# Routing of a mixture of experts planned in two parts, behind an attention kernel

## The chip, the cores and the metric

The kernel runs on one core of a Trainium2 chip. The metric is the device time of one execution in microseconds (us). A core has five engines with an in-order queue each: TensorE (PE, matmuls; PEld is its weight load), VectorE (DVE), ScalarE (ACT), GpSimd (POOL) and SyncE (SP, which here only issues transfers). POOL issues transfers too, with the v loads, the expert weights, and the indirect gathers and scatters.

## The reference

Attention with rotary embedding on 8 batches x 8 heads x 576 tokens x 64, then a dense feed-forward plus, for each of the 4608 tokens, one of 8 experts, chosen by the largest logit and weighted by its probability:

```
q_rot, k_rot = (rotate(q), rotate(k))
scores = scale * np.matmul(q_rot, k_rot.transpose(0, 1, 3, 2))
...
x = np.ascontiguousarray(attn_out.transpose(0, 2, 1, 3)).reshape(B * S, H * D)
y_dense = np.maximum(x @ w1_dense, 0.0) @ w2_dense
expert_idx = np.argmax(x @ w_gate, axis=1)
...
    y_moe[mask] = gate_w[mask, None] * (np.maximum(x[mask] @ w1[e], 0.0) @ w2[e])
return (y_dense + y_moe).astype(np.float32)
```

## The kernel before

**Attention** works on 32 head pairs (NP), four to a batch (HP). In attention() (L466) the loop over pairs i has nine steps t. At step t PE computes the scores of pair i+2 (s1_block, L279) of which DVE takes row maxima (L293, negm), and the shifted scores of pair i (s2_strip, L319) of which ACT takes exponentials (L325). At t = 1, 4 and 6 PE multiplies the exponentials of pair i-1 with ones and with v (av_sums, av_tails, av_main), and DVE scales the result into xf (L365, L373). At t = 2 PE transposes the maxima of pair i+1 (L299, once for each pair), ACT and DVE make two rows mT of them, and SP writes these into the transposed q (L304); the next pair's shifted scores (L314) wait for that. At t = 2 also, rope runs for pair i+4 (stage_rope, L254): on DVE for the first four pairs, then on POOL in four operations (L263 to L266); SP transposes its result (L275). At t = 5 come the loads of q and k (SP), of v (POOL, two heads of each parity at a time), of the feed-forward's weights (POOL, L211): the dense ones at i = 8, one expert's first matrix at every odd i from 11, the second matrices w2e at i = 30 and 31, where the early pool has been given back. At i = 4 route_constants() (L174) builds constants on POOL, three DVE operations read the last of them (L195).

**Routing.** When a batch's four pairs are done, POOL casts xf to xb (L377, L379), PE makes the batch's logits (L389, L398), and gate() (L406) finds the chosen expert as a one-hot table hs and the weight gw on DVE and ACT, for the 5 strips of 128 tokens that a batch has (NS = 40 strips in all). rank() (L425) counts on DVE, with a matmul at its middle (L437, which waits for DVE's cnt, L435), the place of each token among those of its expert, and makes two tables lo for the plan. SP turns xb into rows (x_turn, L456) and writes rows and gw to the DRAM tile xd (x_store, L460); a row has 257 words.

**Plan and feed-forward.** After attention, routing() (L559) places the tokens of each expert in tiles of 128 rows, NT = 43 tiles in all: 80 small matmuls (L592) give for each tile the tokens to take (take_i) and to put (put_i), and woff the expert of each tile. ffn() (L678) runs over groups of 1, 2 and then 4 tiles. fetch() gathers each tile's rows from xd (POOL, L625) and SP transposes them (L628), two groups ahead; dense_in() (L631) computes the dense hidden layer of a group; expert_in, expert_turn and out_tile follow for each tile, the last two one and two tiles later. out_tile() sums the dense part in one PSUM tile and the expert part in another; ACT copies the first (L668), DVE adds the second times gw (L669), POOL scatters the rows to the output (L671).

**Order.** In attention the queues of PE, SP and POOL follow the order as written; those of DVE and ACT are ordered by a planner (L539). Plan: ordered by the planner. In the feed-forward all are as written (L708).

## Time and profile before

| | |
|---|---|
| median of 3 runs | 683.71 us (683.06 to 684.70) |
| the profiled execution | 688.99 us, span 687.3 us, mean granted PE clock 0.897 |
| PE busy | 489.6 us (71%) |
| DVE busy | 429.5 us (62%) |
| ACT busy | 319.0 us (46%) |
| POOL busy | 383.4 us (56%) |
| transfers | 83.50 MB, mean 121 GB/s |
| first L299 / last L299 (PE) | 39.1 us / 463.6 us |
| first dense matmul of the feed-forward (L636) | 514.8 us |

Busy times are sums over the instructions of an engine; the share is of the span. In the slices of the page each digit is the busy share of one fortieth of the span (17.2 us) in tenths, and PEclk is the clock that PE was granted, in tenths of full speed. In a list of waits a line has the waiting instruction, the one waited for, and the total time, the number and the longest of the waits. In a timeline a line has start, duration, engine, line, operation, tiles and shapes, and in brackets the idle time of the engine just before and what ended it. A window gives busy times, the clock, the share of the 16 transfer engines (it can be above 1, as packets overlap) and GB/s.

### The profile page before, as it was taken

To read this page: it belongs to the slowest core of one execution; us is meant where nothing else is said; L and a number is where in the kernel's file an instruction comes from. 1 tells how busy PE (TensorE), PEld (TensorE's weight loads), DVE (VectorE), ACT (ScalarE), POOL (GpSimd) and SP (SyncE) were. 2 spreads that over 40 slices of the span, in tenths; PEclk is the share of its full clock that TensorE was granted. 3 is DMA by queue.
4 is the path that set the end of the run, shared out by engine and by line. 5 is a ranking of instruction groups with operands and counts; after the bars stand their busy time and mean duration, and the time that the engine had idled before them with its cause. 6 is when DMAs were issued, how large, how long until landed. Compare 5 with 4: busy or idle time off the path is not lost. (4 is left out here: it accounts for less than half of the span.)

```text
span 687.3 us, 10849 instructions
## 1 busy us (share of the span) xinstructions
PE 489.6 (71%) x3777; PEld 246.1 (36%) x3777; DVE 429.5 (62%) x737; ACT 319.0 (46%) x644; POOL 383.4 (56%) x340
## 2 busy tenths in 40 slices
PE   0449867387488468738818955884628999999996
PEld 0114434143244234414404432441324444444442
DVE  8767747885987887788797789772341223323233
ACT  2007745265266337526715742763404445444542
POOL 6048959667936936966693595040134545555423
PEclk9999989699889869959977986997758999999999
DMA  8548754379777867577476865279237555546610
GB/s 198 96 91 153 134 108 94 63 164 153 117 146 146 148 127 133 113 122 169 90 149 135 156 115 94 37 122 196 40 81 146 131 139 150 149 125 131 138 62 1
DMA packets 185284, 83.50 MB, mean 121 GB/s; under 512 B 143152, under 2 KB 181552, under 8 KB 185232
## 3 DMA queue, kind: packets, MB, share of 16 engines
q1 hardware_dynamic: 156912, 53.55, 37.5%
q0 software_dynamic: 28320, 29.27, 23.4%
q8 instruction: 31, 0.51, 0.3%
q14 instruction: 21, 0.17, 0.1%
HBM read 52.86 MB, written 16.01 MB: 100 GB/s over the span
## 5 line engine op out<-in xcount | busy, mean ns | idle before, releaser
L293 DVE TENSOR_REDUCE negm<-s 128x1 f32<-128x576 f32 x288 | 210.6, 753 | 79.5 <-PE s L291 62.7
L325 ACT ACTIVATE pm<-s 128x512 f16<-128x512 f32 x288 | 163.3, 594 | 164.4 <-PE s L314 143.7
L291 PE MATMUL s<-qkT 128*128 128x288 bf16 x512 | 116.5, 313 | 34.1 <-DMA qkT<-nat 24.1
L314 PE MATMUL s<-qkT 128*128 128x64 bf16 (+1 forms) x512 | 114.1, 300 | 32.5 <-DMA qkT<-mT 19.3
L263 POOL TENSOR_TENSOR ra<-qk,cosx 128x1152 bf16<-128x1152 f32 x28 | 73.6, 2630 | 89.6 <-DMA qk<-in_k_dram 60.1
L671 POOL DMA_INDIRECT out_dram<-y,put_i x43 | 42.9, 997 | 77.6 <-DVE y L669 77.0
L291 PEld LDWEIGHTS <-qkT 128*128 128x128 bf16 x512 | 42.2, 102 | 89.6 <-issue 46.5
L377 POOL CAST xb<-xf 128x2048 bf16<-128x2048 f32 x8 | 15.1, 1892 | 98.3 <-DVE xf L373 98.3
L669 DVE SCALAR_TENSOR_TENSOR y<-ye,xg,y 128x512 f32<-128x512 f32 x43 | 32.3, 751 | 58.9 <-PE ye L666 33.9
L266 POOL TENSOR_TENSOR nat<-ra,rb 128x1152 bf16<-128x1152 bf16 x28 | 66.3, 2368 | 2.2
L656 DVE COPY he<-tr 128x512 bf16<-128x512 bf16 x43 | 18.2, 423 | 65.7 <-PE tr L654 59.1
L437 PE MATMUL pc<-cnt,tri 128*128 128x8 bf16 x8 | 1.5, 185 | 80.4 <-DVE cnt L435 80.4
L625 POOL DMA_INDIRECT xg<-xd,take_i x43 | 41.4, 963 | 28.1 <-issue 28.1
L314 PEld LDWEIGHTS <-qkT 128*128 128x128 bf16 x512 | 37.5, 100 | 42.8 <-DMA qkT<-mT 17.7
L648 ACT ACTIVATE hn<-pe 128x512 bf16<-128x512 f32 x43 | 25.7, 599 | 49.5 <-PE pe L646 21.2
L636 PE MATMUL pd<-xs,w1d 128*128 128x512 bf16 (+2 forms) x192 | 41.2, 370 | 8.5 <-DMA xs<-xg 7.8
L638 ACT ACTIVATE hd<-pd 128x512 bf16<-128x512 f32 (+2 forms) x48 | 26.4, 553 | 43.2 <-PE pd L636 42.8
L646 PE MATMUL pe<-w1e,xs 128*128 x172 | 45.0, 385 | 1.3 <-issue 1.3
L663 PE MATMUL yd<-w2d,hd 128*128 128x512 bf16 x172 | 44.1, 379 | 0.2
L666 PE MATMUL ye<-w2e,he 128*128 x172 | 44.1, 379 | 0.0
L344 PE MATMUL pz<-pm,ones 128*64 128x512 f16 x320 | 43.7, 406 | 0.0
L344 PE MATMUL px<-pm,v 128*64 128x512 f16 x320 | 41.8, 392 | 0.4 <-ACT lz L351 0.4
(159 smaller groups left out, 771.3 us busy)
## 6 DMA issues: line engine op xcount, KB each, us to landing
qk<-in_q_dram SPq DMA_DIRECT2D x32, 256.0 KB
qk<-in_k_dram SPq DMA_DIRECT2D x32, 256.0 KB
v<-in_v_dram POOLq DMA_DIRECT2D x32, 128.0 KB, 3.6
xd<-natx SPq DMA_DIRECT2D x8, 512.0 KB
w1e<-in_moe_w_dram POOLq DMA_DIRECT2D x8, 512.0 KB, 5.7
w2e<-in_moe_w_dram POOLq DMA_DIRECT2D x8, 512.0 KB, 11.1
qk<-in_q_dram SPq DMA_DIRECT2D x32, 32.0 KB
qk<-in_k_dram SPq DMA_DIRECT2D x32, 32.0 KB
```

The source lines that it names most:

```text
L263: eng.tensor_tensor(a, x, cx, AL.mult)
L266: eng.tensor_tensor(nat[:, :, :, 0:D], a, s, AL.add)
L291: nc.tensor.matmul(ps[:, c, 0:CH], lhsT=qT[:, t * P:(t + 1) * P], rhs=kT[:, k0 + c * CH:k0 + (c + 1) * CH], start=True, stop=True)
L293: nc.vector.tensor_reduce(state["negm", i][:, t:t + 1], ps[:, :, 0:CH], axis=AX.XY, op=AL.max, negate=True)
L314: nc.tensor.matmul(out_ap, lhsT=kT[:, s * P:(s + 1) * P], rhs=qT[:, qa if s < 4 else qb], start=True, stop=True)
L325: nc.scalar.activation(state["pm", i][:, s], ps, AF.Exp, scale=float(scale))
L344: nc.tensor.matmul(out_ap[64 * h:64 * h + 64], lhsT=lhsT, rhs=rhs, start=(n == 0), stop=(n == 4))
L625: nc.gpsimd.indirect_dma_start(out=xg[:, u, :], out_offset=None, in_=xd[:, :], in_offset=bass.IndirectOffsetOnAxis(ap=take_i[:, t:t + 1].b ...
L646: nc.tensor.matmul(ps, lhsT=xs[:, u, dt, :], rhs=w[:, 0, dt, :], start=(dt == 0), stop=(dt == DT - 1))
L663: nc.tensor.matmul(pd, lhsT=hd[:, ft, u], rhs=w2d[:, ft, :], start=(ft == 0), stop=(ft == FT - 1))
L666: nc.tensor.matmul(pe, lhsT=he[:, ft], rhs=w[:, 0, ft, :], start=(ft == 0), stop=(ft == FT - 1))
L671: put = nc.gpsimd.indirect_dma_start(out=out[:, :], out_offset=bass.IndirectOffsetOnAxis(ap=put_i[:, t:t + 1].bitcast(mybir.dt.uint32), ax ...
```

## The change

- logits_sum() only copies a batch's logits into a table lgs. gate() and rank() are replaced by gate_steps() and rank_steps(), each run twice: for the 30 strips of the first six batches, and for the 10 strips of the last two. The gate weight is split in three bf16 parts, which go through the plan's matmuls with the two parts of the token number (NPT = 5) and come out as gp for each tile row; xd loses its column of weights, and x_store two of its four transfers.
- plan_steps() plans T1 = 20 tiles, all full, from the first six batches, and then the remaining 23 from all that is left. The first gate, rank and plan are put into steps of pairs 29 to 32, with the gathers of the first four tiles at (32, 5); the second runs in the feed-forward, two steps to a tile. The matmuls with the tables number 30 and 40 in place of 80.
- Queues: in attention the order of DVE and ACT is now as written too. v is loaded a batch at a time (four transfers at i = 1, 5, ...), an expert's first matrix at every even i from 10, w2e at i = 29 to 31, x_turn of batch b at t = 8 of i = 4b + 6 and x_store at t = 8 of i = 4b + 7 (before: t = 3 of 4b + 5 and t = 7 of 4b + 6); those of the last batch stand behind the loop. The wa pool takes memory from the early pool.
- Feed-forward: groups of 1, 3, 4, 4, 4, 4 and then 4, 4, 4, 4, 4, 3 tiles; dense_in() of the next group is spread over the tiles of this one. The expert's hidden layer is scaled by gp at the ReLU on ACT, both products go into one PSUM tile, and DVE copies it.

```diff
--- before
+++ after
-    VB = 4
+    VB = 2
     v16s = []
     for i in range(VB):
-        t = const_p.tile([P, 2, 10, D], fp16, name=f"v16_{i}")
+        t = const_p.tile([P, HP, 10, D], fp16, name=f"v16_{i}")
...
+    SA = 5 * (B - 2)
+    NA = (B - 2) * S
-    XR = DG // 2 + 1
+    XR = DG // 2
     NT = N // P + E - 1
+    T1 = (NA - E * (P - 1) + P - 1) // P
+    T2 = NT - T1
...
+    lgs = route_p.tile([P, NS, E], f32)
+    groups = ((0, SA), (SA, NS))
...
+    NPT = 5
+    parts = route_p.tile([P, NS, NPT, 1], bf16)
...
-    def stage_v(g):
+    def stage_v(b):
...
+            heads = v[b, a::2]
...
     def logits_sum(b):
...
-        lg = ap.tile([P, 5, E], f32, tag="lg", bufs=1, name="lg")
-        nc.vector.memset(lg[TAIL:P, 4, :], 0.0)
-        nc.vector.tensor_copy(lg[:, 0:4, :], ps[:, 0:4, :])
-        nc.vector.tensor_copy(lg[0:TAIL, 4, :], ps[0:TAIL, 4, :])
-        gate(b, lg)
+        nc.vector.tensor_copy(lgs[:, 5 * b:5 * b + 4, :], ps[:, 0:4, :])
+        nc.vector.tensor_copy(lgs[0:TAIL, 5 * b + 4, :], ps[0:TAIL, 4, :])
...
+    def gate_steps(k, wp):
...
+        def a():
+            nc.vector.tensor_reduce(mx[:, :, 0], lg, axis=AX.X, op=AL.max)
+            nc.vector.tensor_tensor(ex, lg, mx.broadcast_to(sh), AL.subtract)
+        def b():
+            fb = first.rearrange("p j e -> p (j e)")[:, None, :].broadcast_to([P, n // 5, 5 * E])
+            nc.vector.scalar_tensor_tensor(hit.rearrange("p (b j) e -> p b (j e)", j=5),
+                                           in0=ex.rearrange("p (b j) e -> p b (j e)", j=5), scalar=0.0,
+                                           in1=fb, op0=AL.is_equal, op1=AL.mult)
+            nc.scalar.activation(ex, ex, AF.Exp)
+            nc.vector.tensor_reduce(top[:, :, 0], hit, axis=AX.X, op=AL.max)
+            nc.vector.tensor_scalar(top, top, scalar1=0.5, scalar2=None, op0=AL.max)
+        def c():
+            nc.vector.tensor_tensor(hs.rearrange("p e s -> p s e"), hit, top.broadcast_to(sh), AL.is_equal)
+            nc.vector.tensor_reduce(gw, ex, axis=AX.X, op=AL.add)
+            nc.vector.reciprocal(gw, gw)
+        def d():
+            nc.vector.tensor_copy(pt[0], gw)
+            nc.vector.tensor_tensor(gw, gw, pt[0], AL.subtract)
+            nc.vector.tensor_copy(pt[1], gw)
+            nc.vector.tensor_tensor(gw, gw, pt[1], AL.subtract)
+            nc.vector.tensor_copy(pt[2], gw)
+        return [a, b, c, d]
...
+    def rank_steps(k, wp, psum):
...
+        def a():
+            nc.vector.tensor_tensor_scan(run.rearrange("p e s -> p (e s)"),
+                                         keeps[k].rearrange("p e s -> p (e s)"),
+                                         hs.rearrange("p e s -> p (e s)"), 0.0, AL.mult, AL.add)
+            nc.vector.tensor_copy(cnt, run[:, :, n - 1])
+        def b():
+            pc = psum([P, 2, E, 1])
+            nc.tensor.matmul(pc[:, 0, :, 0], lhsT=tri, rhs=cnt, start=True, stop=(k == 0))
+            for x in range(k):
+                nc.tensor.matmul(pc[:, 0, :, 0], lhsT=ones_b, rhs=cnts[x], start=False, stop=(x == k - 1))
+            for x in range(k + 1):
+                nc.tensor.matmul(pc[:, 1, :, 0], lhsT=ones_b, rhs=cnts[x], start=(x == 0), stop=(x == k))
+            st["pc"] = pc
+            nc.vector.tensor_tensor(run, run, pc[:, 0].broadcast_to(sh), AL.add)
+            nc.vector.tensor_tensor(run, run, hs, AL.mult)
+        def c():
+            nc.vector.tensor_reduce(rel, run.rearrange("p e s -> p s e"), axis=AX.X, op=AL.add)
+            nc.vector.tensor_scalar(ri[:, 1], rel, scalar1=-1.0, scalar2=None, op0=AL.add)
+            nc.vector.tensor_scalar(ri[:, 0], ri[:, 1], scalar1=P - 1, scalar2=None, op0=AL.bitwise_and)
+            nc.vector.tensor_scalar(ri[:, 1], ri[:, 1], scalar1=7, scalar2=None, op0=AL.arith_shift_right)
+            nc.vector.tensor_scalar(rf[:, :, 0], ri[:, 0], scalar1=1.0, scalar2=None, op0=AL.add)
+            nc.vector.tensor_copy(qf[:, s0:s1, 0], ri[:, 1])
+        def d(h, nh):
+            r0, r1 = n * h // nh, n * (h + 1) // nh
+            sl = [P, r1 - r0, P]
+            nc.vector.tensor_tensor(oh[:, s0 + r0:s0 + r1], cf[:, None, :].broadcast_to(sl),
+                                    rf[:, r0:r1].broadcast_to(sl), AL.is_equal)
+        nh = (n + 9) // 10
+        return [a, b, c] + [lambda h=h: d(h, nh) for h in range(nh)], st
...
+    def plan_steps(k, wp, psum, st):
...
+        def d(r):
+            m = r.stop - r.start
+            nc.vector.tensor_tensor(on[:, r, 0], cf[:, None, 0:NK].broadcast_to([P, m, NK]),
+                                    h[:, r].broadcast_to([P, m, NK]), AL.is_equal)
+            nc.vector.tensor_tensor(onp[:, r], on[:, r].broadcast_to([P, m, NPT, NK]),
+                                    parts[:, r].broadcast_to([P, m, NPT, NK]), AL.mult)
+        def e(r):
+            if r.start == 0:
+                ps["pt"] = psum([P, NPT, NK])
+            for s in range(r.start, r.stop):
+                nc.tensor.matmul(ps["pt"], lhsT=oh[:, s], rhs=onp[:, s], start=(s == 0), stop=(s == ns - 1))
...
+        cuts = [slice(x, min(x + 15, ns)) for x in range(0, ns, 15)]
+        return ([a] + [lambda x=x: b(x) for x in range(k + 1)] + [c, g] + [lambda r=r: d(r) for r in cuts],
+                [lambda r=r: e(r) for r in cuts], f)
...
     def x_store(b):
         r0 = b * S
-        for src, c0, c1 in ((natx.bitcast(i32), 0, DG // 2), (gw.bitcast(i32), DG // 2, DG // 2 + 1)):
-            nc.sync.dma_start(xd[r0:r0 + MAIN, c0:c1].rearrange("(p j) c -> p j c", j=4), src[:, 0:4, :])
-            nc.sync.dma_start(xd[r0 + MAIN:r0 + S, c0:c1], src[0:TAIL, 4, :])
+        src = natx.bitcast(i32)
+        nc.sync.dma_start(xd[r0:r0 + MAIN, :].rearrange("(p j) c -> p j c", j=4), src[:, 0:4, :])
+        nc.sync.dma_start(xd[r0 + MAIN:r0 + S, :], src[0:TAIL, 4, :])
...
-                    if i % 2 == 0 and i // 2 + 1 < NP // 2:
-                        stage_v(i // 2 + 1)
+                    if i % HP == 1 and i // HP + 1 < B:
+                        stage_v(i // HP + 1)
                     if i == 4:
                         route_constants()
                     if i == 8:
                         load_w(w1d, moe_w1_dense)
                         load_w(w2d, moe_w2_dense)
-                    if i % 2 == 1 and 11 <= i < 11 + 2 * E:
-                        load_w(w1e[:, (i - 11) // 2], moe_w1[(i - 11) // 2])
-                    if i == NP - LA + 1:
+                    if i % 2 == 0 and 10 <= i < 10 + 2 * E:
+                        load_w(w1e[:, (i - 10) // 2], moe_w1[(i - 10) // 2])
+                    if i == NP - LA:
                         early_cm.__exit__(None, None, None)
-                        open_w2e()
-                    if NP - LA + 1 < i <= NP:
-                        for e in range(3 * (i - NP + LA - 2), min(E, 3 * (i - NP + LA - 1))):
-                            load_w(w2e[0][:, e], moe_w2[e])
+                        open_late()
+                        wa = late["wa"]
+                        for x, st in enumerate(gate_steps(0, wa)):
+                            steps[29, 2 * x] = [st]
+                        rk, got = rank_steps(0, wa, attn_sums)
+                        steps[29, 8] = rk[0:1]
+                        steps[30, 2] = rk[1:3]
+                        pl, mm, fin = plan_steps(0, wa, attn_sums, got)
+                        steps[30, 4] = pl[0:3]
+                        steps[30, 5] = pl[3:4]
+                        for x, st in enumerate(rk[3:]):
+                            steps[30, 6 + x] = [st]
+                        for x, st in enumerate(pl[4:]):
+                            steps[31, 1 + 2 * x] = [st]
+                        steps[32, 5] = mm + [fin, fetch_first]
+                    if NP - LA < i <= NP:
+                        for e in range(3 * (i - NP + LA - 1), min(E, 3 * (i - NP + LA))):
+                            load_w(late["w2e"][:, e], moe_w2[e])
+                for st in steps.pop((i, t), ()):
+                    st()
                 if b is not None:
                     if t == 3:
                         logits_part(b)
-                        x_turn(b)
-                    if t == 7:
+                    if t == (7 if i < NP else 4):
                         logits_sum(b)
-                if i >= 6 and (i - 6) % HP == 0:
-                    if t == 1:
-                        rank((i - 6) // HP)
-                    if t == 7:
-                        x_store((i - 6) // HP)
+                if t == 8 and i < NP:
+                    if i >= 6 and (i - 6) % HP == 0:
+                        x_turn((i - 6) // HP)
+                    if i >= 7 and (i - 7) % HP == 0:
+                        x_store((i - 7) // HP)
             if i < NP:
                 s2_tails(i, 0)
                 s2_tails(i, 1)
+        assert not steps
+        x_turn(B - 1)
         x_store(B - 1)
-        rank(B - 1)
...
-    sizes = [1, 2] + [GT] * ((NT - 3) // GT)
+    sizes = [1, 3] + [GT] * ((T1 - 4) // GT)
+    assert sum(sizes) == T1
+    G1 = len(sizes)
+    while sum(sizes) < NT:
+        sizes.append(min(GT, NT - sum(sizes)))
...
+    def fetch(g, pool, tag, bufs):
+        n, t0 = sizes[g], sum(sizes[:g])
+        rows = NA if g < G1 else N
+        m = n if pool is first_p else GT
+        xg = pool.tile([P, m, XR], i32, tag=f"xg{tag}", bufs=bufs, name="xg")
+        xs = pool.tile([P, m, DT, P], bf16, tag=f"xs{tag}", bufs=bufs, name="xs")
+        for u in range(n):
+            t = t0 + u
+            nc.gpsimd.indirect_dma_start(
+                out=xg[:, u, :], out_offset=None, in_=xd[0:rows, :],
+                in_offset=bass.IndirectOffsetOnAxis(ap=take_i[:, t:t + 1].bitcast(mybir.dt.uint32), axis=0))
+            nc.sync.dma_start_transpose(xs[:, u], xg[:, u, :].bitcast(bf16))
+        got.append(xs)
+    def fetch_first():
+        fetch(0, first_p, 0, 1)
+        fetch(1, first_p, 1, 1)
...
-        with tc.manual_schedule(engines={nc.tensor.engine, nc.sync.engine, nc.gpsimd.engine}):
+        with tc.manual_schedule():
...
+            nc.vector.tensor_copy(ident_b, ident_f)
...
-        nc.scalar.activation(hn, ps, AF.Relu)
+        nc.scalar.activation(hn, ps, AF.Relu, scale=gp[:, t:t + 1])
...
-        pd = fpp.tile([P, DG], f32, tag="yd", bufs=1, name="yd")
-        pe = fpp.tile([P, DG], f32, tag="ye", bufs=2, name="ye")
+    def out_tile(t, hd, u, he, e):
+        py = fpp.tile([P, DG], f32, tag="py", bufs=2, name="py")
+        w = late["w2e"][:, bass.ds(e, 1), :, :]
         for ft in range(FT):
-            nc.tensor.matmul(pd, lhsT=hd[:, ft, u], rhs=w2d[:, ft, :], start=(ft == 0), stop=(ft == FT - 1))
-        w = w2e[0][:, bass.ds(e, 1), :, :]
+            nc.tensor.matmul(py, lhsT=hd[:, ft, u], rhs=w2d[:, ft, :], start=(ft == 0), stop=False)
         for ft in range(FT):
-            nc.tensor.matmul(pe, lhsT=he[:, ft], rhs=w[:, 0, ft, :], start=(ft == 0), stop=(ft == FT - 1))
-        y = fp.tile([P, DG], f32, tag="y", bufs=8, name="y")
-        nc.scalar.copy(y, pd)
-        nc.vector.scalar_tensor_tensor(y, in0=pe, scalar=xg[:, u, DG // 2:DG // 2 + 1].bitcast(f32), in1=y,
-                                       op0=AL.mult, op1=AL.add)
+            nc.tensor.matmul(py, lhsT=he[:, ft], rhs=w[:, 0, ft, :], start=False, stop=(ft == FT - 1))
+        y = fp.tile([P, DG], f32, tag="y", bufs=6, name="y")
+        nc.vector.tensor_copy(y, py)
...
+        plan = gate_steps(1, wb)
+        rk, st = rank_steps(1, wb, sums)
+        pl, mm, fin = plan_steps(1, wb, sums, st)
+        plan += rk + pl + mm + [fin]
+        until = sum(sizes[:G1 - 2])
+        per = -(-len(plan) // until)
...
-            xg, xs, n = got[g]
+            n = sizes[g]
             if g + 2 < NG:
-                got.append(fetch(g + 2))
-            hd = dense_in(xs, n)
+                fetch(g + 2, fp, "", 3)
+            dense = dense_steps(g + 1) if g + 1 < NG else []
             for u in range(n):
                 t = sum(sizes[:g]) + u
-                hn, e = expert_in(t, xs, u)
-                todo.append({"t": t, "hd": hd, "u": u, "hn": hn, "e": e, "xg": xg})
+                hn, e = expert_in(t, got[g], u)
+                todo.append({"t": t, "hd": hds[g], "u": u, "hn": hn, "e": e})
+                for st in dense[FT * u // n:FT * (u + 1) // n]:
+                    st()
                 advance()
+                for st in plan[:per]:
+                    st()
+                del plan[:per]
```

## The prediction

> **What bounds the kernel now.** I read the page's busy slices first, then the list of waits, then the timelines of PE, DVE and POOL over one batch, then the windows.
>
> ```profile
> PE   0449867387488468738818955884628999999996
> PEclk9999989699889869959977986997758999999999
> ```
>
> ```profile
> 550.00:600.00 50.00, 49.47 (x271) 23.91 (x269) 16.14 (x28) 23.21 (x40) 26.02 (x27) 1.00 0.54 143
> ```
>
> In the slices PE is dented once every 3.4 slices (57.6 us, one batch of four pairs) up to slice 27, drops to 2 in slice 29, and is at 9 from slice 31; PE's clock dips with it. The second fence is one window (busy PE, PEld, DVE, ACT, POOL; clock; DMA share; GB/s) shows the feed-forward: PE 49.47 of 50 us at full clock, so only fewer or faster matmuls shorten that stage. The waits say what the dents are:
>
> ```profile
> PE pc L437 <- DVE cnt L435: 80.4, 7, 13.8
> ...
> DVE pi L195 <- POOL tok L192: 6.6, 1, 6.6
> ```
>
> PE's in-order queue stands at rank()'s first matmul for 80.4 us in seven waits. One of them, and the last batch but one for comparison:
>
> ```profile
> 293.24 6.25 DVE L419 TENSOR_TENSOR hs<-hit,mx 128x32 f32<-128x32 f32 x1
> 295.43 2.64 POOL L263 TENSOR_TENSOR ra<-qk,cosx 128x1152 bf16<-128x1152 f32 x1
> 301.03 2.28 DVE L432 TENSOR_TENSOR_SCAN run<-keep,h 128x40 f32<-128x40 f32 x1
> 303.57 0.19 PE L437 MATMUL pc<-cnt,tri 128*128 128x8 bf16 x1 [13.80 <-DVE cnt L435]
> ...
> 461.78 0.22 DVE L419 TENSOR_TENSOR hs<-hit,mx 128x32 f32<-128x32 f32 x1
> 463.14 0.18 PE L437 MATMUL pc<-cnt,tri 128*128 128x8 bf16 x1
> ```
>
> The DVE operation on 32 numbers takes 6.25 us while POOL's rope runs and 0.22 us when no rope is left; then PE doesn't wait. What a pair costs is the distance between the L299 transposes, one a pair:
>
> ```profile
> 278.22 0.27 PE L299 MATMUL mps<-ident_f,negm 128*9 128x128 f32 x1
> 304.51 0.42 PE L299 MATMUL mps<-ident_f,negm 128*9 128x128 f32 x1
> 316.52 0.27 PE L299 MATMUL mps<-ident_f,negm 128*9 128x128 f32 x1
> 326.15 0.27 PE L299 MATMUL mps<-ident_f,negm 128*9 128x128 f32 x1
> 335.78 0.27 PE L299 MATMUL mps<-ident_f,negm 128*9 128x128 f32 x1
> ```
>
> Plain pairs take 9.63 us, the pair with the gate and rank 26.3, the one after it 12.0 (PE's clock is still down). Without the wait a pair with logits costs 11.73 (451.90 to 463.63, the quiet one), 2.1 above a plain one. The seam to the feed-forward is the second place:
>
> ```profile
> 477.84 1.01 PE L314 MATMUL s<-qkT 128*128 128x512 bf16 x2 [8.01 <-DMA qkT<-mT]
> 503.91 3.09 PE L592 MATMUL pt<-on,lo 128*128 128x43 bf16 x80 [7.37 <-DVE on L588]
> 508.62 1.06 POOL L625 DMA_INDIRECT xg<-xd,take_i  x1 [15.30 <-issue]
> 514.76 2.09 PE L636 MATMUL pd<-xs,w1d 128*128 128x128 bf16 x16 [7.75 <-DMA xs<-xg]
> ```
>
> PE first loses 8 us to a late mT transfer (x_turn and eight w2e loads are ahead of it), then waits for the plan, then for the gather.
>
> **The change part by part.** The sum is made against the span of the profiled execution, 687.3 us (its time 688.99; the median of the runs, 683.71, is 0.9948 of the span).
>
> *Start.* DVE is now in written order: the first rope operation of pair 2 (1.36 us), which ran in DVE's idle 4.15 us before the first scores, falls behind nine reductions; with ident_b's copy (0.22) the DVE-bound start grows by 1.6. **+1.6.** From then on ACT's and DVE's written order inside a plain pair is the one they have in the trace (reduce, reduce, reduce, mT, two reduces, xf, ...), so this costs nothing in the pairs.
>
> *Pairs.* From the L299 of the second pair (51.40) to that of the last (463.63) are 30 steps, 412.2 us. gate() and rank() leave all of them; logits leave two DVE copies of 0.19 and 0.15. The wait at route_constants goes too: v's four loads no longer stand before it on POOL in pair 4, and its DVE reader stands later in the written order. New: 30 x 9.63 + 7 x 2.1 = 303.6. **-108.6.** The rank waits are 78.2 of it, route_constants some 7.8, the rest is the cold clock after each.
>
> *What hides less then.* A batch shrinks from 57.6 to 40.6 us, and two others must fit into it. POOL: rope 31.2 (10.5 + 9.5 + 5.6 + 5.6), xb casts 2.3, two w1e issues 1.6, four v issues of twice the bytes in place of eight. These bigger issues lie between 0.62 (today's small one) and 0.82 (w1e's, four times the bytes); I take 0.75, 3.0 in all: 38.1, just under 40.6. DMA: share 0.71 of 57.56 us is 40.9 us of all engines, almost one for one. That share isn't a ceiling: 455 to 480 us it is 1.22. Smooth pairs at 9.63 ran at 0.74 (316 to 336), and at 1.06 (150 to 160) one pair took 13.41, 3.8 more. On SP the mT transfer of a pair stands behind the previous transpose, which waits for POOL's rope, then (in one pair a batch) behind x_turn (3.1). Lower bound 0; upper 3.8 for three of the four pairs of the four batches with expert weights, 45. I take 3.8 once (w1d and w2d together, as now) and 0.9 a batch for six batches, nearer to the smooth row since the loads are now spread over even pairs: **+9**.
>
> *Last pairs.* The w2e loads go out two pairs earlier, but x_turn(6) now comes after the last mT in SP's queue: of the 8.0 us wait I let 4 go (bounds 0 and 8); the pair after it ran partly at half clock (ten pz matmuls 2.34 instead of 1.27), 2.3 goes. Gate, rank and plan of 30 strips add some 23 us to DVE from pair 29 on: about 45 operations; 240-element ones at 0.4 (between 0.20 for 40 and 0.47 to 0.75 for 320), three oh of 1280 at 1.6 (twice 0.82), two onp of 1500 at 1.8 (0.77 per 640). From pair 30 no reductions run, so they lie in DVE's idle time (PE holds at most the pc matmul); pair 29 has 3.9 of them beside 7.6 of its own in 11.7: 2 us late. **-4.3** (-4 - 2.3 + 2).
>
> *Seam.* Now from the last tails (488.1) to the first gather (508.62) 20.5 us. New: 30 matmuls (1.5; 80 narrower ones took 3.1 on a cold clock), three DVE operations to take_i (0.6), 0.3 to POOL, 1.5 for DVE being late: 3.9. **-16.6.** The last av, the logits and their copies (some 5 us) now run while the gathers fly.
>
> *Feed-forward.* The matmuls stay (192 + 43 x 16, 43 x 4 transposes). ACT's 43 copies of 0.585 leave, DVE's 0.75 becomes a copy: off the bound, worth 0. Supply is thinner: behind four gathers POOL now casts xb(7) (2.3) and SP turns it (3.1) before the second group of four; today eleven gathers run in a row. PE reaches dense_in of group 2, issued a tile earlier than now, some 5 us before its tiles: +5. The second plan puts some 20 us of DVE work into ten tiles of 3.6 us, of which DVE uses 1.2: it fits but for the bundle of two onp, and the pc matmul waits for a scan queued behind y: +3 (0 to 20). PE starts warm: -1. **+7.**
>
> The second plan also puts DVE operations on SBUF beside POOL's gathers and scatters. The row: POOL issues each in 0.95 to 1.04 us now, beside DVE operations that mostly read PSUM. The Trainium skill, SBUF — State Buffer, section "SBUF: two separate sides", speaks against the change: a DVE operation that holds both ports keeps POOL from writing descriptors. By that rule as many as 20 us of issues would be held; by the row none; gathers go out two groups (some 29 us) ahead, so the sum is the same by both.
>
> Sum: 687.3 + 1.6 - 108.6 + 9 - 4.3 - 16.6 + 7 = 575.4; x 0.9948 = **572 us**.
>
> **The rivals.**
> 1. *DMA becomes the bound.* For: 40.9 us of transfers in a 40.6 us batch, and the 13.41 pair. Against: shares of 1.2 occur. At the upper bound, 45 instead of 9: 611 span, 608.
> 2. *The second plan stalls PE.* For: in-order queues, he copies stand behind onp. Against: DVE has two thirds of the stage free. All 20 us exposed instead of 3: 592 span, 589.
> 3. *The wait only moves*: POOL lags, its last ropes fall on pair 29, and the bulk gates are stretched like L419. For: POOL has only 2.5 us of slack a batch. Against: the last rope is issued at pair 27. One stall of 13.8: 589 span, 586.
> 4. *Slower: POOL becomes the bound through SP.* If rope cannot keep up, SP holds transpose and mT, and PE loses the excess in each batch. It decides from 40.6 us of POOL work a batch, and makes the kernel slower than before from 112 / 7 = 16 us more. At 20 more: 575.4 + 140 = 715 span, 712. For: POOL is at 38.1. Against: its operations last the same in every pair (L263 2.63, DVE busy or not).
>
> **How the numbers follow.** Forecast 0.70, rival 1 0.14, 2 0.06, 3 0.06, 4 0.04. The low end leaves out DMA (9), the mT wait (4), supply (5) and plan (3) and some of the lateness: 575.4 - 21 = 554, with 3 for DVE's lag 551, x 0.9948 = 548. The high end is rival 1 with the whole mT wait kept: 615 span, 612. What one can tell from no change is 0.2%, 1.4 us; only rival 4 reaches there or beyond (at 16 us a batch it would be no change): faster 0.95, same 0.01, slower 0.04.
>
> **What would show it.** Right: no wait of PE for cnt before pair 29; L299's copies 9.6 to 9.9 apart, 11.7 to 12.5 with logits; first gather within 5 us of the plan's matmuls; PE's first dense matmul before 400 us; PE near 98% after the first ten us of feed-forward. Wrong: pairs of 11 and more with waits on qkT or nat (rival 1), PE waits on cnt, onp or tr in the first ten tiles (2), L431 to L470 of microseconds (3), POOL over 95% busy and SP waiting for nat (4).

## The result and the profile after

The changed kernel takes 597.38 us (median of 4 runs, 596.31 to 599.77), the kernel before, beside it, 683.38 (4 runs, 681.74 to 684.70): a ratio of 0.8747, 95% interval 0.8714 to 0.8781. The forecast was 572, the range 548 to 612. The profiled execution took 596.31 us, its span is 594.6, against the 575.4 of the sum: 19.2 us are to be found. The other 6 of the 25 us between 572 and 597.38 are the step from span to time: the profiled execution of the kernel before was 0.8% longer than the median of its runs, that of the changed kernel was the shortest of its four.

From the page of the changed kernel, the busy slices of PE, its clock and the transfer engines (a slice is now 14.9 us):

```profile
PE   0254998887998997987997999766689999999995
PEclk9999999998898897989899899897799999999998
DMA  8824955789988798999999853992925464456610
```

The deep dents of before are gone from the pairs (slices 4 to 24); shallow ones, at 7, are left, and the seam at 6 and 7. Its list of waits (waiting instruction, what it waited for, total us, number, longest):

```profile
POOL xb L390 <- DVE xf L386: 39.2, 7, 16.4
...
PE s L327 <- DMA qkT<-mT: 28.2, 9, 9.2
...
POOL ra L276 <- DMA qk<-in_k_dram: 19.8, 7, 5.5
...
PE pd L758 <- DMA xs<-xg: 7.6, 2, 5.2
...
PE pz L357 <- DVE xf L378: 3.7, 1, 3.7
...
PE sums L478 <- DVE cnt L473: 1.5, 1, 1.5
```

The 80.4 us of PE waiting for cnt are 1.5 now, in the second plan. In their place PE waits for the mT rows: 9.2 us once in the start, and 19 us later. The mps transposes, one a pair, show where (timeline of PE):

```profile
262.69 0.27 PE L312 MATMUL mps<-ident_f,negm 128*9 128x128 f32 x1
271.91 0.27 PE L312 MATMUL mps<-ident_f,negm 128*9 128x128 f32 x1
...
281.85 0.38 PE L327 MATMUL s<-qkT 128*128 128x512 bf16 x1 [3.15 <-DMA qkT<-mT]
```

A plain pair takes 9.22 us (262.69 to 271.91), 0.41 less than before; the next mps comes at 285.54, 13.63 later, with 3.15 of waiting and PE partly on a lower clock after it. What SP had done meanwhile (timeline of SP):

```profile
269.17 0.57 SPq L246 DMA_DIRECT2D qk<-in_q_dram  x1
269.81 0.70 SPq L248 DMA_DIRECT2D qk<-in_q_dram  x1
270.55 0.58 SPq L246 DMA_DIRECT2D qk<-in_q_dram  x1
271.18 1.26 SPq L248 DMA_DIRECT2D qk<-in_q_dram  x1
272.48 0.59 SPq L610 DMA_DIRECT2D xd<-natx  x1
273.12 0.51 SPq L611 DMA_DIRECT2D xd<-natx  x1
273.73 1.60 SPq L317 DMA_DIRECT2D qkT<-mT  x2
275.44 5.88 SPq L288 DMA_TRANSPOSE qkT<-nat  x1
```

mT of this pair was complete at 273.15 on DVE. Its two issues, of 2.2 KB each, follow a store of 576 KB and loads of as much on the same queue, POOL issued a weight load (w1e) at 271.28, and PE got its rows 6.5 us after the issue ended. The transpose issued next took 5.88 us of SP where a quiet one takes 2.7. About one pair in each batch with weight loads has such a wait, and the batches show it (windows from one mps to the one four pairs later: length, busy PE, PEld, DVE, ACT, POOL; clock, DMA share, GB/s):

```profile
191.50:237.98 46.48, 40.28 (x352) 19.62 (x351) 29.74 (x51) 29.86 (x63) 39.16 (x26) 0.90 0.84 166
237.98:285.54 47.56, 39.72 (x351) 19.50 (x350) 29.65 (x51) 29.58 (x62) 36.42 (x25) 0.93 0.98 161
...
330.46:370.23 39.77, 36.70 (x352) 18.92 (x350) 30.02 (x53) 29.21 (x62) 23.16 (x17) 1.00 0.54 93
```

The first two carry expert weights, the last none. Between attention and feed-forward (timelines of PE and POOL):

```profile
402.72 2.34 PE L357 MATMUL pz<-pm,ones 128*64 128x512 f16 x10 [3.67 <-DVE xf L378]
...
405.53 1.62 PE L573 MATMUL sums<-onp,oh 128*128 128x100 bf16 x30
...
408.16 1.06 POOL L728 DMA_INDIRECT xg<-xd,take_i  x1 [33.44 <-DVE off L584]
...
414.02 1.01 PE L758 MATMUL pd<-xs,w1d 128*128 128x128 bf16 x8 [2.41 <-DMA xs<-xg]
...
428.12 1.86 PE L758 MATMUL pd<-xs,w1d 128*128 128x512 bf16 x4 [5.18 <-DMA xs<-xg]
```

The first gather comes 3.4 us after the last tails (404.81), where it took 20.5; the third group's tiles hold PE for 5.18 us.

### The profile page after: what moved, and what is told of

Its sections match the earlier page's. It is cut to its first block, busy times and chain, and to the rows that moved or that the text cites. A ratio compares the mean times of both kernels' runs of the same rounds, so it can differ in the third digit from the quotient of the medians.

```text
span 594.6 us, 10561 instructions
## 1 busy us (share of the span) xinstructions
PE 486.0 (82%) x3738; PEld 241.0 (41%) x3756; DVE 346.7 (58%) x653; ACT 294.9 (50%) x595; POOL 364.7 (61%) x305
## 5 line engine op out<-in xcount | busy, mean ns | idle before, releaser
L306 DVE TENSOR_REDUCE negm<-s 128x1 f32<-128x576 f32 x288 | 207.6, 748 | 85.9 <-PE s L304 76.4
L304 PE MATMUL s<-qkT 128*128 128x288 bf16 x512 | 113.3, 306 | 31.7 <-DMA qkT<-nat 25.4
L790 POOL DMA_INDIRECT out_dram<-y,put_i x43 | 42.8, 996 | 80.8 <-DVE y L789 57.6
L728 POOL DMA_INDIRECT xg<-xd,take_i x43 | 43.2, 1004 | 46.2 <-DVE off L584 33.4
L789 DVE COPY y<-py 128x512 f32<-128x512 f32 x43 | 29.7, 690 | 49.4 <-PE py L787 45.5
L770 ACT ACTIVATE hn<-pe,gp 128x512 bf16<-128x512 f32 x43 | 29.5, 686 | 54.3 <-PE pe L767 53.4
L357 PE MATMUL pz<-pm,ones 128*64 128x512 f16 x320 | 50.6, 456 | 3.7 <-DVE xf L378 3.7
L758 PE MATMUL pd<-xs,w1d 128*128 128x512 bf16 (+2 forms) x192 | 46.7, 375 | 8.2 <-DMA xs<-xg 7.6
L787 PE MATMUL py<-w2e,he 128*128 x171 | 43.9, 379 | 0.0
L785 PE MATMUL py<-w2d,hd 128*128 128x512 bf16 x164 | 42.4, 379 | 0.4
L357 PEld LDWEIGHTS <-ones 128*64 128x64 f16 x640 | 28.6, 119 | 34.2 <-issue 24.0
L277 POOL TENSOR_TENSOR rb<-qk,sinx 128x576 bf16<-128x576 f32 x28 | 39.4, 1406 | 0.0
```

The source lines that it names most:

```text
L304: nc.tensor.matmul(ps[:, c, 0:CH], lhsT=qT[:, t * P:(t + 1) * P], rhs=kT[:, k0 + c * CH:k0 + (c + 1) * CH], start=True, stop=True)
L306: nc.vector.tensor_reduce(state["negm", i][:, t:t + 1], ps[:, :, 0:CH], axis=AX.XY, op=AL.max, negate=True)
L357: nc.tensor.matmul(out_ap[64 * h:64 * h + 64], lhsT=lhsT, rhs=rhs, start=(n == 0), stop=(n == 4))
L758: nc.tensor.matmul(ps[:, 0:n], lhsT=w1d[:, dt, ft * P:(ft + 1) * P], rhs=xs[:, 0:n, dt, :], start=(dt == 0), stop=(dt == DT - 1))
L785: nc.tensor.matmul(py, lhsT=hd[:, ft, u], rhs=w2d[:, ft, :], start=(ft == 0), stop=False)
L787: nc.tensor.matmul(py, lhsT=he[:, ft], rhs=w[:, 0, ft, :], start=False, stop=(ft == FT - 1))
```

## The experiments

One length is compared throughout: the 28 steps from the second mps transpose to the thirtieth, so the start and the two last pairs, with the bulk gates, stand outside. Without any wait they are 22 plain pairs of 9.22 and 6 with logits of 12.08, 275.3 us. Both numbers come from one execution of a kernel, unless a number of runs is given; the four of the changed kernel spread over 3.5 us, and the executions stand on several chips (the kernel before took 685.26 beside e1 to e4, 690.31 beside e5 to e8, 684.78 beside e9 to e11). Differences of some 5 us between two rows are not to be read; a wait that is there or gone in a pair is.

| kernel | second mps at | 28 steps | time |
|---|---|---|---|
| before | 51.40 | 390.9 | 683.38 |
| before, gates last (e4) | 51.41 | 357.4 | 675.02 |
| before, written order (e5) | 51.89 | 396.3 | 694.92 |
| before, gates last, written order (e6) | 51.88 | 303.1 | 647.59 |
| changed | 54.28 | 306.7 | 597.38 |
| changed, expert weights late (e1) | 54.08 | 288.6 | 585.97 |
| changed, mT on ACT's queue (e2) | 50.28 | 349.9 | 637.80 |
| changed, rows behind mT (e3) | 52.88 | 300.7 | 589.81 |
| changed, weights spread (e7) | 53.70 | 311.0 | 602.51 |
| changed, no rows in the pairs (e9) | 52.66 | 285.7 | 579.49 |
| changed, start alone (e10) | 40.70 | 309.5 | 586.83 |
| combined (e8) | 46.34 | 287.5 | 568.12 |
| plan earlier (e11) | 45.49 | 286.9 | 565.40 |

### Which part of the change emptied the pairs

Gates and ranks behind the pairs, nothing else (e4):

```diff
-        gate(b, lg)
...
-                    if t == 1:
-                        rank((i - 6) // HP)
...
+        for b in range(B):
+            gate(b)
+            rank(b)
+            gw_store(b)
```

> The kernel before with its eight gate and rank steps (and the stores of gate weights) taken out of the pairs and run one after another behind them; nothing else of the change, so DVE and ACT are still ordered by the planner. The theory of the prediction: the 80.4 us of PE waits for cnt are all of what the change gained in the pairs; the 30 steps fall from 412.2 to some 304 to 331 us, a plain pair stays at 9.63. The rival: the wait only moves (another wait of 5 us or more in each batch takes its place), steps above 350. The time: 684 less 80 to 108, plus eight times some 6 to 8 us behind the pairs, 625 to 665.

Measured: 357.4 (378.5 over the 30 steps), the time 675.02; five pairs of 21 to 23 us are left, in five of the six batches: the rival's case. PE waits 46.2 us in eight waits for DVE's maxima. The timelines of POOL, DVE and PE of this run show why:

```profile
217.00 1.39 POOL L267 TENSOR_TENSOR rb<-qk,sinx 128x576 bf16<-128x576 f32 x1
218.47 2.36 POOL L268 TENSOR_TENSOR nat<-ra,rb 128x1152 bf16<-128x1152 bf16 x1
...
223.44 2.65 POOL L265 TENSOR_TENSOR ra<-qk,cosx 128x1152 bf16<-128x1152 f32 x1
226.01 1.42 POOL L266 TENSOR_TENSOR rb<-qk,sinx 128x576 bf16<-128x576 f32 x1
...
216.56 1.89 DVE L411 TENSOR_TENSOR ex<-lgs,mx 128x40 f32<-128x40 f32 x1
218.38 0.74 DVE L295 TENSOR_REDUCE negm<-s 128x1 f32<-128x576 f32 x1
219.04 1.83 DVE L414 SCALAR_TENSOR_TENSOR hit<-ex,first 128x40 f32<-128x40 f32 x1
220.91 0.20 DVE L416 TENSOR_REDUCE mx<-hit 128x5 f32<-128x40 f32 x1
221.15 6.37 DVE L419 TENSOR_TENSOR hs<-hit,mx 128x32 f32<-128x32 f32 x1
...
229.80 0.69 PE L289 MATMUL s<-qkT 128*64 128x288 bf16 x4 [7.25 <-DVE negm L295]
```

The gates are written behind the loop, but the planner of DVE's order put them back among the reductions of pair 14; PE waits for the maxima instead of for cnt. The two other edits of the kernel before, e5 and e6, are one word of the call that sets the order, without and with the gates moved:

```diff
-        with tc.manual_schedule(engines={nc.tensor.engine, nc.sync.engine, nc.gpsimd.engine}):
+        with tc.manual_schedule():
```

> The kernel before with one thing changed: in attention DVE and ACT keep the written order instead of the planner's. Gates and ranks stay in the pairs. Theory: the plain pair of 9.63 us comes from the planner's putting two row-maximum reductions ahead of mT on DVE, so that the PSUM slot of mps comes free late and PE waits 0.32 us for it; in written order a plain pair takes 9.22. Gate and rank still stand on DVE beside POOL's rope, so one pair in four still takes over 20 us, and the 30 steps stay above 390 (before 412.2), the time above 665. Rival: the order is what the change gained in the pairs; then the steps fall under 350 here.

> The kernel before with gates and ranks behind the pairs, as in the run before, and DVE and ACT in written order, so that the planner can't pull the gates back between the reductions, as it did there (hs 6.37 us inside pair 14, PE waiting 7.25 us for negm). Theory: without gates on DVE beside the rope no pair is over 16 us; plain 9.22, logits 12 to 12.5; the 30 steps 300 to 335 against 412.2 before and 418.6 less 40 there; the gates and ranks behind the pairs cost 8 times 5 to 8 us, so the time is 620 to 650. Rival: POOL or the queue of v (eight small issues a batch) holds the pairs anyway; then pairs above 16 us remain and the steps stay above 350.

Measured: order alone makes a plain pair 9.22 and the pairs with gate and rank 24 to 28 us; 30 steps 419.0, the time 694.92. Gates moved and held there by the order: no pair over 14.7 us, 30 steps 325.3, 28 steps 303.1, the time 647.59; both theories hold where they give numbers. So the 28 steps lose 33.5 us by moving the gates, nothing by the order (5.4 more), and 87.8 by both: the change needs its written order to keep the gates out. Its new places for v, weights and rows did not add to that, its 306.7 are 3.6 more.

The emptied pairs are only a part of the gain, though. In e6 the wait has moved behind them, where eight gates and ranks run one after another:

```profile
PE pc L437 <- DVE cnt L435: 43.2, 8, 5.8
```

From the last mps to the first gather e6 takes 85.8 us, the kernel before 45.0, the changed kernel 22.9, and with pairs about as long e6 is some 50 us slower than the changed kernel. That the changed kernel doesn't pay this price is the other half of the change: gates and ranks for 30 strips at once, and a plan in two parts. What each of these two is worth alone was not run.

The 0.41 of a plain pair, first from the timelines of DVE and PE of the kernel before, then of the changed one:

```profile
326.14 1.42 DVE L293 TENSOR_REDUCE negm<-s 128x1 f32<-128x576 f32 x2 [0.98 <-PE s L291]
327.48 0.27 DVE L302 TENSOR_TENSOR mT<-mps,mT 9x128 bf16<-9x128 f32 x1
...
328.06 0.38 PE L311 MATMUL s<-qkT 128*64 128x512 bf16 x1 [0.32 <-ACT pm L325]
```

```profile
307.05 0.76 DVE L306 TENSOR_REDUCE negm<-s 128x1 f32<-128x576 f32 x1 [1.01 <-PE s L304]
308.03 0.28 DVE L315 TENSOR_TENSOR mT<-mps,mT 9x128 bf16<-9x128 f32 x1 [0.22 <-ACT mT L314]
...
308.49 0.38 PE L324 MATMUL s<-qkT 128*64 128x512 bf16 x1
```

The planner had two reductions ahead of mT. mT ends at 327.75, 1.60 after its mps (326.15), and the strip at 328.06 waits 0.32; in written order it stands behind one reduction, ends 1.25 after the mps (307.06), and PE does not wait. mps and the strips share two PSUM buffers (tag s2), so this is the slot's release; that the release and not pm is what it waited for is argued from the names, not shown by a run. That the order gives 9.22 is shown by e5.

### What the once-a-batch wait is made of

Two theories: density (the batch has more to transfer than fits) and queue order (mT stands behind other things in SP's queue). Expert weights out of pairs 10 to 24 (e1):

```diff
-                    if i % 2 == 0 and 10 <= i < 10 + 2 * E:
-                        load_w(w1e[:, (i - 10) // 2], moe_w1[(i - 10) // 2])
...
+                    if i == NP - LA:
+                        for e in range(E):
+                            load_w(w1e[:, e], moe_w1[e])
```

> The changed kernel with the eight loads of the experts' first matrices taken out of pairs 10 to 24 and issued together at pair 28; the feed-forward will start late, so only the pairs are to be read. In the changed kernel the 30 steps between the mps transposes take 331.0 us, the four batches that carry these loads 44.5, 46.5, 47.6 and 44.9 us, the next 39.8, and PE waits 28.2 us for mT rows. Theory density (too many transfers in a batch): those four batches come to 40 to 41 us each, the mT waits after the start to under 4 of 19 us, the steps up to pair 27 shorten by some 20 us. Theory queue order (mT stands behind the stores of rows and the loads in SP's queue): without these loads the stores and the q and k loads still stand ahead of mT, so most of the waits stay and the batches stay above 43 us.

Measured: the four batches 39.9, 41.1, 41.0 and 42.8 us, mT waits 10.0 after the start, steps up to pair 27 shorter by 18.1. The pairs go density's way (the waits fall less: to 10.0 where it said under 4), and although all eight loads now fall on the last pairs (the last two of the 30 steps take 17.6 and 15.3 us), the time is 585.97, 11.4 less.

mT issued by ACT (e2), which should have freed it from SP's queue (the issues are held back by one step; two of the lines):

```diff
-            nc.sync.dma_start(qT[D + r:D + r + 1, :].rearrange("o (c p) -> o c p", p=P), mT[:, r])
+                nc.scalar.dma_start(qT[D + r:D + r + 1, :].rearrange("o (c p) -> o c p", p=P), mT[:, r])
```

> The changed kernel with the two transfers of mT issued from ACT's queue, one strip later, instead of SP's. Theory queue order: mT no longer stands behind loads, stores and transposes, so the waits of PE for mT rows (19 us after the start) fall under 4 us and the 30 steps from 331 to 312 to 318 us, less what two issues a pair cost ACT (each 0.6 to 0.8 us on SP; up to 0.5 us on a plain pair of 9.22, because ACT is busy 7.3 of these). Theory density: the transfer engines have as much to move as before (share 0.84 to 0.98 in the four loaded batches), so the delay only moves to other waits (rope for k, the transposes), and the loaded batches stay within 1.5 us of 44.5, 46.5, 47.6 and 44.9.

Measured: worse than either theory, 349.9. A plain pair takes 10.25 us, 1.03 more, and six times ACT stands up to 8.7 us. One of them, ACT:

```profile
179.94 0.73 ACTq L318 DMA_DIRECT2D qkT<-mT  x1
...
188.42 0.73 ACTq L318 DMA_DIRECT2D qkT<-mT  x1
189.20 0.60 ACT L340 ACTIVATE pm<-s 128x512 f16<-128x512 f32 x1 [8.72 <-DMA qkT<-nat]
```

The second row's issue waited until a transpose of another pair had landed, with the exponentials behind it in ACT's in-order queue. What ties the two together no row shows; this run tells the theories apart in nothing.

The rows' turn and store behind mT and transpose (e3):

```diff
+                if t == 2:
+                    if i >= 7 and (i - 7) % HP == 0:
+                        x_turn((i - 7) // HP)
+                    if i >= 8 and (i - 8) % HP == 0:
+                        x_store((i - 8) // HP)
...
-                if t == 8 and i < NP:
-                    if i >= 6 and (i - 6) % HP == 0:
-                        x_turn((i - 6) // HP)
-                    if i >= 7 and (i - 7) % HP == 0:
-                        x_store((i - 7) // HP)
```

> The changed kernel with the turn and the store of a batch's rows moved in SP's queue from just ahead of the next mT to just behind mT and transpose of the next pair. Theory queue order: the worst waits (3.1 to 3.7 us, once a batch, each behind a store of 576 KB) go, the 30 steps fall by 10 to 15 us from 331, mT waits after the start from 19 to 8 or less. Theory density: same steps within 4 us, the waits fall on other pairs.

Measured: 6.0 us less, between the two; mT waits 14.6 after the start. The pairs with a wait still take 12.4 to 13.9 us. In one of them mT's issue ended at 269.45, with no store ahead of it, and PE had its rows at 274.38, 4.9 us later: the store is not what makes most of the wait. Half the weights and no change of the rows (e7):

```diff
-                    if i == 8:
-                        load_w(w1d, moe_w1_dense)
-                        load_w(w2d, moe_w2_dense)
-                    if i % 2 == 0 and 10 <= i < 10 + 2 * E:
-                        load_w(w1e[:, (i - 10) // 2], moe_w1[(i - 10) // 2])
+                    if i % HP == 2 and i // HP + 1 < E:
+                        load_w(w1e[:, i // HP + 1], moe_w1[i // HP + 1])
...
+    def early_w():
+        seen = ap.tile([P, 1], f32, tag="seen", bufs=1, name="seen")
+        nc.gpsimd.tensor_copy(seen, state["negm", 0][:, 0:1])
+        load_w(w1d, moe_w1_dense)
+        load_w(w2d, moe_w2_dense)
+        load_w(w1e[:, 0], moe_w1[0])
...
+            if i == 0:
+                early_w()
```

> The changed kernel with the weight loads spread: the two dense matrices and the first expert's in the start, behind pair 0's first row maxima (there the transfer share is 0.01 to 0.56), the other seven one a batch at pairs 2, 6, ... 26. Theory density: a batch with one load instead of two lies between the loaded ones (44.5 to 47.6 us) and the unloaded (39.8): 40 to 42.5 us each, the 30 steps fall from 331 to 305 to 316, the time from 597 to 574 to 583. Rival, that any weight load makes the once-a-batch wait: batches stay above 44, steps above 325.

Measured: 311.0 with one load a batch instead of two, not shorter than the changed kernel; the time, 602.51, is 0.873 of the before beside it, as the changed kernel's is. That is density's miss, and the batches over 44 us are what the rival, that any weight load makes the wait, had said. The load of a batch now stands at the pair whose end has the turn of rows, and the bad pair has moved there. Its SP and PE:

```profile
213.04 6.36 SPq L288 DMA_TRANSPOSE qkT<-nat  x1
...
222.13 3.97 SPq L604 DMA_TRANSPOSE natx<-xb  x1
226.21 1.65 SPq L317 DMA_DIRECT2D qkT<-mT  x2
...
229.09 0.59 PE L327 MATMUL s<-qkT 128*128 128x512 bf16 x1 [4.79 <-DMA qkT<-mT]
```

mT was complete at 218.75 on DVE. It was issued 7.5 us later, behind a transpose (6.36 us beside the weight load), four loads of q and k (2.5) and the turn (3.97); PE had it 1.2 us after. Here the wait is SP's issue time, in the changed kernel's pair above it was the time to landing.

So the coincidence of a weight load with the rows was tried by taking the rows away and leaving the weights (e9; this kernel leaves out the turns of all batches but the first and the last, so its output is computed from wrong rows; the times of its pairs are what it is for):

```diff
-                    if i >= 6 and (i - 6) % HP == 0:
-                        x_turn((i - 6) // HP)
-                    if i >= 7 and (i - 7) % HP == 0:
-                        x_store((i - 7) // HP)
+                    if i == 6:
+                        x_turn(0)
+                    if i == 28:
+                        for x in range(B - 1):
+                            x_store(x)
```

> The changed kernel without the turns of rows in the pairs: rows are turned once, for the first batch, and seven stores of these same rows stand together at pair 28 (the gathered rows are thus not the batch's own; weights and everything else as in the changed kernel). Compared over the 28 steps from the second mps transpose to the thirtieth, which take 306.7 us in the changed kernel, 288.6 without the weight loads, 300.7 with turns and stores behind mT, 301.0 to 311 with the weights spread; 22 plain pairs of 9.22 and 6 with logits of 12.08 would be 275.3. Theory coincidence: the once-a-batch wait needs both a weight load (it stretches SP's transposes from 2.7 to 6 us and shares the transfer engines) and the turn and store of rows (4.2 us of SP's queue in a batch, 576 KB ahead of mT); with the weights but no rows the 28 steps take 278 to 291. Theory density: 1.1 MB of rows a batch less, the weights stay: 295 to 303. If weights alone make the wait: above 303.

Measured: 285.7, the coincidence's number. Of the 31.4 us over 275.3, 18.1 go when only the weights leave (e1) and 21.0 when only the rows do: together more than the whole, so a good part of it needs both. Pair by pair this is plainer. The four pairs with an expert's load and the longest wait, 17.8 us above quiet ones in the changed kernel, are quiet (9.21 and 9.22) in e1 and in e9 alike: there the wait needs both, and e7's rival falls. The pair after the two dense loads stays in both (15.34 in e1, 13.27 in e9, 14.55 in the changed kernel): these two make it without rows. The waits for mT, 9.2 of them in the start:

```profile
PE s L327 <- DMA qkT<-mT: 17.3, 5, 9.2
```

### Better starts and a combination

Start alone (e10): ropes of pairs 2 and 3 on POOL, and mT of pair 0 issued ahead of the transpose of pair 3:

```diff
-        eng = nc.vector if i < LA else nc.gpsimd
+        eng = nc.vector if i < 2 else nc.gpsimd
...
+            stage_rope(i + 2)
             for t in range(9):
                 s1_block(i, t)
-            stage_rope(i + 2)
+                if i == 1 and t == 3:
+                    shift_rows(0)
             stage_transpose(i + 2)
-        shift_rows(0)
```

> The changed kernel with only the start of the combined one: ropes of pairs 2 and 3 on POOL, which idles there, and mT of pair 0 ahead of the transpose of pair 3. The second mps transpose comes at 46 to 48 us as in the combined kernel (46.3; 54.3 in the changed one). Theory that POOL's being late (each first rope operation after a late k load, then the transpose, then mT behind it in SP's queue) makes the waits: with POOL ahead by a pair the 28 steps fall from 306.7 to 290 to 298. Theory coincidence of weights and rows: they stay at 303 to 309, and the time is 597 less 8, 587 to 591.

Measured: the second mps at 40.70, 13.6 us sooner and sooner than expected, the 28 steps unchanged (309.5), 586.83 in all. POOL's lead does not help the pairs. The edits of e3, e7 and e10 together, and in the feed-forward the last batch's turn behind the gathers of the third group (e8):

```diff
-        x_turn(B - 1)
-        x_store(B - 1)
...
                 fetch(g + 2, fp, "", 3)
+            if g == 0:
+                x_turn(B - 1)
+                x_store(B - 1)
```

> The spread loads, the row turns and stores behind mT, and in the start the ropes of pairs 2 and 3 on POOL, which is idle from 13.5 to 46.5 us, instead of DVE (2 x 3.6 us of a DVE-bound start), with mT of pair 0 issued ahead of the transpose of pair 3; the last batch's turn behind the gathers of group 2. Expected: the second mps transpose at 43 to 48 us instead of 54.3, the 30 steps 300 to 312 (331), the first dense wait of group 2 (5.2 us) down to 1 to 3; the time 560 to 573. If transfers bound the start, the second mps stays above 51 and the time is 570 to 580.

Measured: second mps 46.34 (5.6 later than e10's; e12 below, without the three early weight loads, has 41.29), 28 steps 287.5 (311.7 over the 30), wait for the third group's tiles 2.77, time 568.12 (2 runs), ratio to before 0.8275 (0.8058 to 0.8493): all as expected. The batches (windows):

```profile
150.16:191.41 41.25, 36.62 (x351) 18.74 (x350) 29.67 (x51) 29.42 (x63) 37.29 (x25) 1.00 0.89 176
...
232.98:274.11 41.13, 38.08 (x351) 19.17 (x350) 29.53 (x51) 29.53 (x63) 36.09 (x24) 0.96 0.88 172
```

and those of e7, with the same one load a batch:

```profile
186.99:233.66 46.67, 38.74 (x351) 19.28 (x350) 29.73 (x51) 29.61 (x63) 36.47 (x24) 0.94 0.77 155
233.66:278.85 45.19, 38.54 (x351) 19.33 (x350) 29.58 (x51) 29.48 (x62) 36.50 (x23) 0.95 0.79 156
```

The faster batches have the higher share, 0.88 against 0.78: as much is moved in less time, so the transfer engines are not what bounds e7's. Of the 19.2 us that e8's steps gain, its parts alone give 6.0 (rows) and nothing (spread weights +4.3, start +2.8); which two of them suffice wasn't run.

With the routing's constants in POOL's idle start, the gates one pair and the plan's matmuls one pair earlier (e11):

```diff
     def attention():
+        route_constants()
...
-                    if i == 4:
-                        route_constants()
...
-                            steps[29, 2 * x] = [st]
+                            steps[28, 5 + x] = [st]
...
-                        steps[29, 8] = rk[0:1]
-                        steps[30, 2] = rk[1:3]
+                        steps[29, 1] = rk[0:1]
+                        steps[29, 8] = rk[1:3]
...
-                        steps[32, 5] = mm + [fin, fetch_first]
+                        steps[31, 6] = mm + [fin, fetch_first]
```

> The combined kernel with the constants of the routing made in POOL's idle start instead of at pair 4, the gates a pair earlier (pair 28, just after the last rope), the count's matmul at the last step of pair 29 and the plan's matmuls and first gathers in pair 31 instead of behind it. From the combined kernel: pairs 4 and 5 took 13.87 and 13.60 where 9.22 and 12.08 are quiet, so 6 us there; PE's wait for DVE's xf (2.3), the cold pz (1.1) and the wait for the first tiles (2.4 to 2.8) go: 5 to 6. 568 less 8 to 12: 554 to 562. If the bulk gates meet the last rope, hs takes over 3 us instead of 0.59 and pair 28 or 29 is 3 to 6 us longer: 560 to 566.

Measured: 565.40 us (6 runs, 561.71 to 569.92), 0.8265 of before, interval 0.8225 to 0.8304: faster than both kernels, above the expected 554 to 562, and not told apart from e8. From the last mps the first gather comes 15.8 us on (23.1 in e8) and the first dense matmul 23.0 (28.9); pairs 4 and 5 are quiet (9.22, 12.07). But pairs 7 and 8 now take 12.26 and 10.53, and PE, sooner at the third group, waits longer:

```profile
394.36 1.86 PE L762 MATMUL pd<-xs,w1d 128*128 128x512 bf16 x4 [5.08 <-DMA xs<-xg]
```

Last, the weights out of the start, at pairs 1, 3 and 5, and the third group of four tiles cut in two (e12):

```diff
+                    if i in (1, 3, 5):
+                        load_w(*((w1d, moe_w1_dense), (w2d, moe_w2_dense), (w1e[:, 0], moe_w1[0]))[i // 2])
...
-    sizes = [1, 3] + [GT] * ((T1 - 4) // GT)
+    sizes = [1, 3, 2, 2] + [GT] * ((T1 - 8) // GT)
```

> The kernel of the run before with no weight loads in the start (with them the second mps transpose came at 45.5 to 46.3 us, without them at 40.7): the dense matrices and the first expert's go to pairs 1, 3 and 5, ahead of the first rows, the others one a batch as there; and the feed-forward's third group of four tiles is cut in two groups of two (PE waited 5.1 us for all four). Expected: second mps at 40 to 42, the 28 steps 284 to 290 (286.9), the wait for the third group 1 to 3 us: 565.4 less 4.5 and 2 to 4, 557 to 559, 555 to 562 with the spread of that run's executions. If weight loads alone, without rows, make waits in pairs 1 to 6, the 28 steps are above 292 and the time is 562 or more.

Measured: 569.37 us (567.04 to 576.06), beside a before of 689.61 on its chip, 0.8255 (0.8224 to 0.8287): the same as e11, a miss. The start came as expected (41.29), the wait for tiles moved two groups on, whole (5.09 us at the first group of four, 425.82). Its profiled execution was the longest of the six, so its pairs are not compared.

## Why the prediction was right, and where it was off

The forecast's mechanism holds, and so does its sign: gates on DVE beside POOL's rope held PE, the change takes them out of the pairs (-81.3 us of the span), and the seam gives the second, smaller part (-22.1). One thing the forecast took for granted: that a gate written behind the pairs stays there. e4 shows that it doesn't under the planner; the written order, priced at nothing in the pairs, is what keeps it there. By its own terms, in us of the span:

| term | forecast | measured |
|---|---|---|
| start, to the second mps | +1.6 | +2.9 |
| second to last mps (303.6, +9 for what hides less, +2 for DVE's lag) | 314.6 | 331.0 |
| last mps to first gather (45.0 - 4 - 2.3 - 16.6) | 22.1 | 22.9 |
| first gather to the end (178.7 + 7) | 185.7 | 186.4 |

The differences, 1.3, 16.4, 0.8 and 0.7, are the 19.2. The 16.4 are three errors: 7.0 too many for pairs without waits, 22.4 too few for what hides less, 0.9 too few in the last two steps. That the first takes away a third of the second is luck.

*Start.* From DVE's first reduction to the second mps it is 28.22 us instead of 26.56: the 1.7 of the written order, as reckoned. The other 1.2 lie ahead of the first scores and are not shown to be the change's: e3 and e9, with the same start, have the second mps at 52.88 and 52.66.

*Pairs without waits.* "This costs nothing in the pairs" was said of DVE's and ACT's written order; it gains 0.41 in a plain pair. 30 steps without waits are 23 x 9.22 + 7 x 12.08 = 296.6 instead of 303.6. The logits pair is 2.86 above a plain one, not 2.1: the plain pair fell, the logits pair (11.73 in the quiet pair of before) did not.

*What hides less.* This is the mis-sized term. It was put at 9 us and measured 31.4 (306.7 less 275.3; both lie in the bounds of 0 and 45). The nearest rows were read as one wait of 3.8 for the dense weights and 0.9 a batch; what the trace has is 5.3 us at the pair of the dense weights, 3.2 to 5.2 at one pair of each of the four batches with expert weights (17.8 in all), and 1.5 to 3.4 at four other pairs (8.1). So the 0.9 a batch, 5.4 in all, is what was mis-sized: 26 us stand in its place. The place was in the text ("the mT transfer of a pair stands behind the previous transpose, ... then ... behind x_turn"), and the loads' spreading over even pairs was taken as a relief. It is the other way: at every fourth pair a load meets the rows, and e9 and e1 show that either alone makes no wait there. Which of the transfers delays which is not shown: the wait was SP's issue time in e7, the time to landing in the changed kernel.

*Rival 1*, density, at 45, came a good two thirds true in size, and its sign, pairs of 11 us and more with waits on qkT, came too; but not in kind: e7 with half the load is no faster, e8 at a higher share is faster. *Rival 3* failed: the bulk hs on 240 elements took 0.59 us and the scan 0.64, since no rope is left. *Rival 4*: POOL was busy 35.2 to 39.2 us in the four batches with expert weights, against 38.1 reckoned, and xb's cast found 16.4 us of idle time on it at the last; v's issues took 0.80, 0.63, 0.76 and 0.64 against 0.75. It did not bound.

*Last pairs and seam.* The mT wait, of which 4 were kept, was 0.73. Earlier w2e loads, one of the two reasons given, did not come: all eight are issued some 1.6 us before the next-to-last mps in both kernels (450.11, 368.71). What is left is that x_turn, 11.82 us of SP ahead of mT before, now stands behind it. DVE's lateness, reckoned at 1.5, was a wait of 3.67 for xf behind three oh (4.27) and two on and onp (4.4), and a cold pz (2.34 instead of 1.27) behind it: two errors that cancel, so that this term fits within 0.8 us is luck.

*Feed-forward.* The thin supply was sized right, 5.18 where 5 was said, the second plan held PE 1.5 us on cnt where 3 was said (*rival 2* failed), and PE was busy 98% of the time from 434 to 580 us. The first dense matmul came at 414, not before 400, by the 17.7 us that the start and the pairs were late.

*The rule weighed against the row.* The Trainium skill, SBUF — State Buffer, section "SBUF: two separate sides", was weighed for POOL's transfers in the feed-forward. The trace agrees in kind: two gathers beside the plan's oh and onp on DVE took 1.69 and 1.70 us, a third 1.36, and the other 40 stay at 0.94 to 1.06; 1.9 us in all, and PE waits for no tiles there, where up to 20 were the rule's bound. The same section says that DVE operations with two SBUF inputs and POOL's reads exclude each other for whole instructions, and e4's fence agrees from DVE's side, but there the hs operation waited through more than one instruction of POOL.

## What to carry to other kernels

A small operation that takes microseconds beside another engine's long ones is a wait in disguise; before moving it, ask which order keeps it from being put back, since a planner can pull work from behind a loop into its idle slots, as it did in e4; then ask who pays for the operation in its new place, as PE does in e6. When a batch gets shorter, don't price the transfers by their share alone: list, for the small transfer that the critical engine needs, what stands ahead of it in its queue in each pair, and look for the pair where two big ones meet. A wait for a supply can move to a later group, whole, when the first is cut, as in e12.
